# Loading w_down in 7 KB runs, with the gate and up weights read at a column step of 14

## Chip, cores, metric

One core of one Trainium2 chip. The metric is the device time of the whole kernel in microseconds (us), of which every kernel has several runs. Before: 640.87 us median of 4 runs.

## The reference

Two decode layers with shared weights: a GQA attention block over a cache of 8192 positions, and a SwiGLU FFN, run twice. Cut to what matters:

```python
B, D, F = 4, 512, 1792
Hq, Hkv, Sk, Dh = 32, 8, 8192, 128
def _A_ref(x, k_cache, v_cache, wq, wo): ...      # attention; the kernels here read 256 MB, nearly all of it k_cache and v_cache
def _B_ref(x, w_gate, w_up, w_down):
    g = silu(x @ w_gate)                           # w_gate, w_up: [512, 1792]
    u = x @ w_up
    return (g * u) @ w_down                        # w_down: [1792, 512]
x = x + _A_ref(layernorm(x), ...)
x = x + _B_ref(layernorm(x), ...)
x = x + _A_ref(layernorm(x), ...)
x = x + _B_ref(layernorm(x), ...)
```

## The kernel before

The kernel streams both caches once per layer through 11 buffers of 1 MB, except for pieces that it keeps from the first layer for the second, and computes beside the stream. The weights stay in SBUF after one load. Layer 1 is taken batch by batch, so its FFN runs four times inside the stream (each time for all four columns, of which one batch is ready), and once more at the end, for layer 2: five FFNs. A planner in the host code orders the steps of each engine from estimated durations; the order of the loads is a fixed, tuned list.

```python
P, KT, FO = 128, D // 128, F // 128                # 128, 4, 14
def ffn_mm(w_sb, wname, f0, f1, deps, tag):        # gate, and up in two halves
    def fn():
        bk = pbk(tag)
        for fo in range(f0, f1):
            for kt in range(KT):
                op("pe", lambda e: e.matmul(ps[:, bk * BW + (fo - f0) * B:bk * BW + (fo - f0 + 1) * B],
                                            lhsT=w_sb[:, kt, fo * P:(fo + 1) * P],          # stationary: 128 columns
                                            rhs=xnT[:, kt * B:(kt + 1) * B],                # moving: 4 columns
                                            start=(kt == 0), stop=(kt == KT - 1)), ...)
    return PL.add("pe", 0.0295 * KT * (f1 - f0) + 0.05, fn, deps + [...], CHAIN, take=tag, n=2 * KT * (f1 - f0))

def dn(h=h):                                       # down projection, per half
    ...  matmul(..., lhsT=wd_sb[:, fo, nq * P:(nq + 1) * P], rhs=hT[:, fo * B:(fo + 1) * B], ...)

# the loads: what goes where, and the planner's estimate in us
wspec[f"wd{k}"] = (wd_sb[:, fs, :], B_w_down.rearrange("(fo p) n -> p fo n", p=P)[:, fs, :], 2.6)   # k = 0, 1
ORDER = "... a150 wo2 a151 a171 a170 wo3 wu1 wd0 wd1 a160 a161 ..."     # a, b, c: V loads (c: kept for both layers); K: a K load
```

Row f of w_down sits at partition f mod 128, group f // 128, so each partition gets 14 separate rows of 1 KB. hidden(f) must sit at the same place, which is what contiguous blocks of 128 gate and up columns give.

## Time and profile before

| | before |
|---|---|
| time, median of 4 | 640.87 us (639.56 to 641.52) |
| span of the profiled run | 637.9 us |
| bytes read from HBM, rate over the span | 256.1 MB, 402 GB/s |
| TensorE busy, VectorE busy | 63%, 64% |
| DMA packets, of them under 2 KB | 41124, 9816 |

In 36 of the 40 slices of the span the stream moves 400 to 422 GB/s. In few places the rate falls, as in the window 185 to 190 us with its 213 GB/s. The prediction shows the lines. One more is needed that it does not show, the time from issue to landing of all the loads into the stream's buffers (the view of one tile; us, shortest, median, longest):

```profile
DMA to landing us min/median/max: 5.0/10.5/28.1
```

The shortest, 5.0 us, is the first load of the kernel (issued at 0.74 us), which finds nothing ahead of it. So of the median only some 5.5 us is queue, an estimate from these two numbers.

### The profile page before, as it was taken

How to read it: one execution, taken by the hardware profiler on the slowest of the kernel's cores; microseconds unless marked ns; L12 is line 12 of the kernel's file. 1: busy time of each engine (PE TensorE's matmuls, PEld its weight loads, DVE VectorE, ACT ScalarE, POOL GpSimd, SP SyncE). 2: the span in 40 equal slices, each digit the busy share in tenths (PEclk: the TensorE clock that was granted, in tenths of full speed). 3: DMA queues.
4: the chain of work that ended last, by engine and by line, in shares of the span. 5: the costliest groups of instructions: out<-in, count | busy, mean ns of one | idle time of the engine just before them, and what ended most of it. 6: DMA issues, size and time to landing. Idle time of an engine off the chain costs nothing.

```text
span 637.9 us, 18599 instructions
## 1 busy us (share of the span) xinstructions
PE 401.5 (63%) x8657; PEld 202.0 (32%) x8657; DVE 405.2 (64%) x612; ACT 40.2 (6%) x106; POOL 1.8 (0%) x8
## 2 busy tenths in 40 slices
PE   0376454375686655678565575677656776866676
PEld 0231221123542131145331241343421244721355
DVE  6386853464236958776579765466667864499732
ACT  1000200002000020000100100000100020000200
POOL 1000000000000000000000000000000000000000
PEclk9985585565556686665677677567585578577685
DMA  8999999999989999999999999999999999999991
GB/s 362 420 418 407 407 418 420 418 421 400 388 354 422 420 418 420 421 418 404 417 414 418 420 419 421 419 409 411 417 420 420 403 420 420 420 416 420 421 415 42
DMA packets 41124, 257.31 MB, mean 403 GB/s; under 512 B 3924, under 2 KB 9816, under 8 KB 11096
## 3 DMA queue, kind: packets, MB, share of 16 engines
q1 hardware_dynamic: 41048, 256.14, 97.8%
q8 instruction: 67, 1.10, 0.7%
q14 instruction: 9, 0.07, 0.0%
HBM read 256.12 MB, written 0.00 MB: 402 GB/s over the span
## 4 chain that ended last, share of the span: by engine, by line
DMA 64%; PE 16%; DVE 13%; SPq 3%; issue 2%; ACT 0%
DMA pool<-in_A_k_cache_dram 45%; DMA pool<-in_A_v_cache_dram 12%; DVE pool L589 9%; PE ps L605 8%; DMA wq_sb<-in_A_k_cache_dram 5%; PE ps L746 4%; SPq L92 3%; DMA wq_sb<-in_A_v_cache_dram 3%; PE ps L467 1%; DVE negm L624 1%; DVE wq_sb L589 1%; PE ps L792 1%; PE ps L664 1%; PE ps L845 1%; DVE ps L773 1%
## 5 line engine op out<-in xcount | busy, mean ns | idle before, releaser
L589 DVE STREAM_TRANSPOSE pool<-pool 128x2048 uint32<-128x2048 uint32 x116 | 267.1, 2308 | 88.4 <-DMA pool<-in_A_k_cache_dram 87.9
L605 PE MATMUL ps<-pool,qpad 32*32 32x512 bf16 x3840 | 197.4, 548 | 130.8 <-DVE pool L589 125.6
L605 PEld LDWEIGHTS ps<-pool,qpad 32*32 32x32 bf16 x3840 | 55.5, 110 | 248.4 <-DVE pool L589 185.8
L746 PE MATMUL ps<-pool,pp 128*32 128x256 bf16 x1952 | 100.5, 362 | 37.6 <-DMA pool<-in_A_v_cache_dram 28.9
L746 PEld LDWEIGHTS ps<-pool,pp 128*32 128x32 bf16 x1952 | 56.2, 120 | 76.3 <-DMA pool<-in_A_v_cache_dram 34.9
L773 DVE STREAM_TRANSPOSE ps<-ps 128x256 f32<-128x256 f32 x63 | 28.8, 457 | 67.4 <-PE ps L746 67.1
L628 ACT ACTIVATE pp<-ps,negm 128x512 bf16<-128x512 f32 x32 | 21.6, 686 | 322.8 <-DVE negm L624 300.5
L709 PE MATMUL ps<-oT,wo_sb 128*128 128x4 bf16 x640 | 22.4, 166 | 11.3 <-DVE oT L777 8.4
L709 PEld LDWEIGHTS ps<-oT,wo_sb 128*128 128x128 bf16 x640 | 20.0, 102 | 24.8 <-DVE oT L777 15.8
L624 DVE TENSOR_REDUCE negm<-ps 128x1 f32<-128x512 f32 x32 | 19.9, 683 | 12.4 <-PE ps L605 12.4
L467 PE MATMUL ps<-xnT,wq_sb 128*128 128x4 bf16 x640 | 18.3, 166 | 12.8 <-DMA wq_sb<-in_A_wq_dram 11.5
L467 PEld LDWEIGHTS ps<-xnT,wq_sb 128*128 128x128 bf16 x640 | 17.7, 104 | 15.3 <-DMA wq_sb<-in_A_wq_dram 11.6
L589 DVE STREAM_TRANSPOSE wq_sb<-wq_sb 128x2048 uint32<-128x2048 uint32 x8 | 18.5, 2312 | 1.8 <-DMA wq_sb<-in_A_k_cache_dram 1.8
L605 PE MATMUL ps<-wq_sb,qpad 32*32 32x512 bf16 x256 | 11.8, 492 | 9.1 <-DVE wq_sb L589 9.1
L664 PE MATMUL ps<-ident,pp 128*128 128x128 bf16 x128 | 15.4, 300 | 2.5 <-DVE oT L777 1.1
L453 ACT ACTIVATE lnv<-var,eps_sb 128x4 f32<-128x4 f32 x10 | 3.0, 297 | 221.5 <-DVE var L448 221.5
L664 PEld LDWEIGHTS ps<-ident,pp 128*128 128x128 bf16 x128 | 11.9, 137 | 9.6 <-DVE selw L684 2.9
L775 DVE TENSOR_REDUCE osum<-ps 128x4 f32<-128x32 f32 x63 | 12.1, 192 | 2.2
L777 DVE TENSOR_TENSOR oT<-osum,invL 128x4 bf16<-128x4 f32 x63 | 10.6, 169 | 2.1
L673 ACT ACTIVATE pp<-ps 128x1024 bf16<-128x1024 bf16 x8 | 8.2, 1024 | 30.1 <-PE ps L664 30.1
L845 PE MATMUL ps<-hT,wd_sb 128*128 128x4 bf16 x280 | 8.6, 166 | 1.8 <-issue 1.1
L653 DVE TENSOR_SCALAR pp<-pp,alpha 128x512 bf16<-128x512 bf16 x32 | 9.0, 344 | 1.1 <-ACT alpha L646 1.1
(68 smaller groups left out, 143.4 us busy)
## 6 DMA issues: line engine op xcount, KB each, us to landing
pool<-in_A_k_cache_dram SPq DMA_DIRECT2D x116, 1024.0 KB, 10.2
pool<-in_A_v_cache_dram SPq DMA_DIRECT2D x101, 1024.0 KB, 10.8
wq_sb<-in_A_k_cache_dram SPq DMA_DIRECT2D x8, 1024.0 KB, 14.8
wq_sb<-in_A_v_cache_dram SPq DMA_DIRECT2D x5, 1024.0 KB, 16.2
wq_sb<-in_A_wq_dram SPq DMA_DIRECT2D x1, 4096.0 KB, 20.0
wo_sb<-in_A_wo_dram SPq DMA_DIRECT2D x4, 1024.0 KB, 15.5
wg_sb<-in_B_w_gate_dram SPq DMA_DIRECT2D x2, 896.0 KB, 19.2
wu_sb<-in_B_w_up_dram SPq DMA_DIRECT2D x2, 896.0 KB, 16.9
```

The source lines that it names most:

```text
L92: ins = self.eng[engname].dma_start(out_ap, in_ap)
L467: op("pe", lambda e: e.matmul(ps[:, bk * BW + h * B:bk * BW + (h + 1) * B], lhsT=wq_sb[:, kt, h * Dh:(h + 1) * Dh], rhs=xnT[:, kt * B:(kt ...
L589: op("dve", lambda e: e.transpose(v, v), reads=keys, writes=keys)
L605: op("pe", lambda e: e.matmul(ps[32 * c:32 * (c + 1), a * BW:(a + 1) * BW], lhsT=qpad[rows, qbuf, es_, g, :], rhs=ap[h][rows, :, es_ // 2, ...
L624: op("dve", lambda e: e.tensor_reduce(negm[:, q, a:a + 1], bank(a), AX.X, ALU.max, negate=True), reads=[f"pb{a}"], writes=[f"negm{q}_{a}"])
L628: op("act", lambda e: e.activation(pblk(q)[:, :, a, :], bank(a).rearrange("p (t j) -> p t j", j=32), ACTF.Exp, bias=negm[:, q, a:a + 1], s ...
L664: op("pe", lambda e: e.matmul(stg[:, t * P:(t + 1) * P], lhsT=pp[:, q, blk * P:(blk + 1) * P], rhs=ident[:], is_transpose=True, start=True ...
L709: op("pe", lambda e: e.matmul(ps[:, OPJ * BW + nq * B:OPJ * BW + (nq + 1) * B], lhsT=wo_sb[:, h, nq * P:(nq + 1) * P], rhs=oT[:, l, h, :], ...
L746: op("pe", lambda e: e.matmul(ps[32 * n:32 * (n + 1), bk * BW:bk * BW + 256], lhsT=pp[:, q, col:col + 32], rhs=v[:, 8 * f:8 * (f + 1), 32 ...
L773: op("dve", lambda e: e.transpose(blk, blk), reads=[f"pb{bk}"], writes=[f"pb{bk}"])
L775: op("dve", lambda e: e.tensor_reduce(osum[:], diag, AX.X, ALU.add), reads=[f"pb{bk}"], writes=["osum"])
L845: op("pe", lambda e: e.matmul(ps[:, bk * BW + nq * B:bk * BW + (nq + 1) * B], lhsT=wd_sb[:, fo, nq * P:(nq + 1) * P], rhs=hT[:, fo * B:(fo ...
```

## The change

The intent is fewer, longer DMA runs. If row f of w_down goes to partition f // 14, group f mod 14, each partition's share is one piece of 14 KB, loaded in two runs of 7 KB. The hidden activations must then be numbered the same way, so output partition p of group fo needs column p*14 + fo of the gate and up weights: the stationary operand is read with a step of 14 columns, 28 bytes.

```diff
-                                                    lhsT=w_sb[:, kt, fo * P:(fo + 1) * P],
+                                                    lhsT=w_sb[:, kt, bass.ds(fo, P, step=FO)],
...
-            wspec[f"wd{k}"] = (wd_sb[:, fs, :], B_w_down.rearrange("(fo p) n -> p fo n", p=P)[:, fs, :], 2.6)
+            wspec[f"wd{k}"] = (wd_sb[:, fs, :], B_w_down.rearrange("(p fo) n -> p fo n", p=P)[:, fs, :], 2.2)
```

## The prediction

> **What bounds the kernel now.** I read four views in this order: the page's slices and its chain that ended last, the windows by stage, the timeline of the engines around the first and the last FFN, and the queue's issues.
>
> The page first: the DMA digits are 9 in nearly every slice, and the chain is mostly DMA.
>
> ```profile
> DMA  8999999999989999999999999999999999999991
> ...
> HBM read 256.12 MB, written 0.00 MB: 402 GB/s over the span
> ...
> DMA 64%; PE 16%; DVE 13%; SPq 3%; issue 2%; ACT 0%
> ```
>
> So the kernel streams 256 MB and is bound by that stream. The digit line has two breaks: an 8 in slice 11 (175 to 191 us), and the last slice. Elsewhere, compute can be late by several microseconds without moving the end: the K loads take 10.2 us from issue to landing (page, part 6), about four loads of 2.5 us in flight. The windows show the stream's rate in an ordinary stretch, in the stretch with the 1 KB runs of w_down and of the last part of wo, and in the break (columns: window, length, busy us and count of PE, PEld, DVE, ACT, POOL, then granted clock, DMA share, GB/s):
>
> ```profile
> 158.00:169.00 11.00, 7.71 (x186) 6.00 (x174) 2.83 (x14) 0.52 (x3) 0.00 (x0) 0.50 1.07 369
> 200.00:211.00 11.00, 7.16 (x151) 2.37 (x152) 10.66 (x8) 0.00 (x0) 0.00 (x0) 0.64 1.01 422
> 185.00:190.00 5.00, 4.61 (x83) 1.77 (x90) 3.19 (x4) 0.00 (x0) 0.00 (x0) 0.50 0.61 213
> ```
>
> Two places matter for this change. One is the loads of w_down, issued at 156.9 and 158.3 us, when the stream runs at 369 instead of 422 GB/s. The other is every place where an FFN lies on the path. There are five FFNs (four batches of layer 1, one at the end); the last is after the last load and wholly on the path. Its lines in the timeline (start, duration, both us):
>
> ```profile
> 630.26 1.65 PE L792 MATMUL ps<-xnT,wg_sb 128*128 128x4 bf16 x56 [0.49 <-DVE xnT L442]
> 631.78 1.63 PE L792 MATMUL ps<-xnT,wu_sb 128*128 128x4 bf16 x56
> 631.95 0.22 DVE L812 TENSOR_TENSOR gs<-ps,rstd 128x56 f32<-128x56 f32 x1 [1.48 <-PE ps L792]
> 633.25 0.22 DVE L829 TENSOR_TENSOR us<-us,eneg 128x56 f32<-128x56 f32 x1
> 633.50 0.28 DVE L837 TENSOR_TENSOR hT<-us,ps 128x28 bf16<-128x28 f32 x2
> ```
>
> The reader sees a gate of 56 matmuls in 1.65 us, 29.5 ns each, then the up projection beside the vector chain of the SiLU. Up ends at 633.41, the vector chain at 633.47: they finish together, so whatever lengthens up by more than 0.1 us lengthens the end.
>
> The first FFN (batch 0) lies just before the break. There the query of layer 1, batch 0 is made; all buffers hold keys that wait for it, so the loads run dry:
>
> ```profile
> 166.88 1.81 PE L792 MATMUL ps<-xnT,wg_sb 128*128 128x4 bf16 x56 [0.18 <-DVE m L447]
> 169.10 0.89 PE L792 MATMUL ps<-xnT,wu_sb 128*128 128x4 bf16 x28 [0.40 <-DVE gs L812]
> 170.52 0.91 PE L792 MATMUL ps<-xnT,wu_sb 128*128 128x4 bf16 x28 [0.54 <-DVE hT L837]
> 171.70 0.88 PE L845 MATMUL ps<-hT,wd_sb 128*128 128x4 bf16 x27 [0.28 <-DVE hT L837]
> 173.71 0.93 PE L845 MATMUL ps<-hT,wd_sb 128*128 128x4 bf16 x29 [1.12 <-issue]
> 174.90 1.04 PE L746 MATMUL ps<-pool,pp 128*32 128x256 bf16 x16 [0.26 <-DVE xx L861]
> 176.48 1.04 PE L746 MATMUL ps<-pool,pp 128*32 128x256 bf16 x16 [0.54 <-DMA pool<-in_A_v_cache_dram]
> ```
>
> Its slack: 1.12 us of waiting for nothing shown in the down projection, and 0.54 us for a load of V.
>
> [...] A step of 14 bf16 is 28 bytes[...]. No stationary operand of this trace steps that far (the widest is the identity of L480, step 2), so the trace doesn't show the penalty. [...]
>
> **The change, part by part.**
>
> *w_down's loads.* It removes 1792 runs of 1 KB (14 per partition) and adds 256 of 7 KB; the bytes stay 1.835 MB. At 369 GB/s they take 4.97 us, at 422 they take 4.35 us: 0.6 us less. They are in a full stream, so what follows comes 0.6 us sooner. The author's own plan expects 2 x 0.4 us; I keep 0.6.
>
> *Strided weights.* No instruction is added; 5 x 112 = 560 loads of gate and up weights read 28 bytes apart. The down projection, with its rows renumbered the same way, still reads contiguous columns. [...]
> - Last FFN: [...] less the slack of 0.07: **+2.9 us**, all on the path.
> - First FFN: [...] the first half of up runs beside the vector chain, free; the second half starts after hT[...]. The 1.12 us in the down projection and the 0.54 us for V take perhaps 1.0 of it: **+1.2 us** into the break.
> - The other three: [...] against some 10 us of loads in flight: 0. The fourth lets the wq buffer take loads (issue at 557.98), but the stream stays full there.
>
> *The plan.* The order of instructions is computed from estimated times, and the load time entered for w_down falls from 2.6 to 2.2. Everything behind it in the plan may be ordered a little differently. I can't say the sign: +-1 us, mean 0; the order of loads is fixed.
>
> Sum: 640.5 - 0.6 + 2.9 + 1.2 = 644.0 us.
>
> **The rivals.**
>
> 1. *Stride is free.* Weight loads keep 29.5 ns[...]. [...] Then only the DMA gain is left: 640.5 - 0.6 = 639.9 us.
>
> 2. *Doubling, as above*: 644.0 us.
>
> [...]
>
> 4. *The DMA gain is lost in the break.* If batch 0's query comes no sooner, loads that land 0.6 us earlier only run dry 0.6 us earlier: gain 0. For it: the 2 us of missing transfer there (5 us at 213 of 422 GB/s, so 2.5 us). Against it: the wait for V at 176.48 is a wait for that stream. It moves each of the above up by at most 0.6.
>
> **Range and chances.** I give 0.33 to the free stride, 0.55 to doubling, 0.12 to worse. The middle of these, with the DMA gain partly lost, is 643.5 us. The range from 639.2 (free stride, kind plan) to 648.5 (doubling with 2 us more in the break and an unkind plan) should hold 8 times in 10. Faster by 2% would need 627.7 us; the DMA part can't give 13 us, so 0.01. Slower by 2% is above 653.3 us: 0.07. Within 2%: 0.92.
>
> **What would show each step right or wrong.** DMA packets fall from 41124 by 1536 to about 39588, and the window around 158 to 169 us rises from 369 towards 390 GB/s (w_down is some half of it, wo stays at 1 KB). The gate of the last FFN, 56 matmuls, takes 1.65 us if the stride is free[...]; down must keep 1.65. Time from the gate's start to hT in the last FFN, now 3.24 us, grows by 2.9. The break after 185 us gets deeper by about 1 us. The prediction fails if the weight load's cost is not near a factor of two[...], or if the replanned order moves the stream by more than 1 us elsewhere.

The marked cuts took out what no trace shows: a paragraph on how weight loads work, the working of the terms for the strided loads that rested on it, with the added time of the three FFNs in between, what was said for and against the first rival, the third rival (the stride costs about four times), and the test figures that came from these. The sum came to 640.5 - 0.6 + 2.9 + 1.2 = 644.0 us. Of it, +2.9 for the last FFN and +1.2 for the first (where gate and the second half of up were to become longer, and the waits to take 1.0 of that) come from an assumption, that the strided load takes about twice as long; no trace of the kernel before shows it. Without these two terms the sum is 639.9 us.

## The result

650.55 us (648.78 to 652.42, 4 runs) against 640.87: slower by 1.54%, with an interval of 1.19 to 1.89%. A ratio here is the mean time of one kernel's fast runs over that of the other's fast runs of the same rounds, so it isn't quite the ratio of the medians quoted. The time lies 2 us above the predicted range.

Instruction for instruction the two kernels are the same on TensorE, VectorE, ScalarE and GpSimd; only the two loads differ in shape. The smaller number given to the planner moved nothing.

The page of the changed kernel (the DMA digits are tenths of busy time in 40 slices of 16 us, GB/s is the stream's rate in the same slices):

```profile
DMA  8999999999979999999999999999999999999990
GB/s 360 420 417 408 406 418 420 418 420 394 418 298 422 421 420 418 421 399 392 408 412 417 421 419 420 419 400 358 422 405 419 420 421 419 364 413 421 420 407 12
DMA packets 39589, 257.33 MB, mean 398 GB/s; under 512 B 3924, under 2 KB 8024, under 8 KB 9560
...
DMA 60%; PE 25%; DVE 12%; issue 2%; SPq 1%; ACT 0%; DVEq 0%
```

The packets fell as predicted. The chain of work that ended last now has 25% TensorE in place of 16%. The digit of slice 11 is 7 in place of 8; the other holes don't reach the digits, but the row of GB/s has them: counted from 0, slices 17, 18, 27 and 34 (the FFNs of batches 1, 1, 2 and 3) moved 399, 392, 358 and 364, where the page before has 418, 404, 411 and 420. The windows of the same stretches (columns as in the prediction; the last is GB/s):

```profile
158.00:169.00 11.00, 8.04 (x165) 6.49 (x158) 2.60 (x12) 0.50 (x2) 0.00 (x0) 0.50 1.04 397
...
185.00:190.00 5.00, 4.23 (x100) 1.91 (x97) 2.90 (x4) 0.00 (x0) 0.00 (x0) 0.51 0.39 118
```

w_down's stretch rose from 369 to 397 GB/s, and the break fell from 213 to 118. The last FFN in the timeline (start, duration in us):

```profile
635.67 3.52 PE L792 MATMUL ps<-xnT,wg_sb 128*128 128x4 bf16 x56 [0.49 <-DVE xnT L442]
639.05 3.50 PE L792 MATMUL ps<-xnT,wu_sb 128*128 128x4 bf16 x56
...
640.52 0.22 DVE L829 TENSOR_TENSOR us<-us,eneg 128x56 f32<-128x56 f32 x1
...
642.59 0.18 DVE L837 TENSOR_TENSOR hT<-us,ps 128x28 bf16<-128x28 f32 x1 [1.43 <-PE ps L792]
```

Gate and up take twice as long. Up now ends 1.8 us after the vector chain, which waits for it. From the gate's start to the end of the second hT it is 7.10 us in place of 3.52: 3.6 us more. The first FFN:

```profile
166.91 3.49 PE L792 MATMUL ps<-xnT,wg_sb 128*128 128x4 bf16 x56 [0.18 <-DVE m L447]
170.81 1.81 PE L792 MATMUL ps<-xnT,wu_sb 128*128 128x4 bf16 x28 [0.40 <-DVE gs L812]
172.97 1.84 PE L792 MATMUL ps<-xnT,wu_sb 128*128 128x4 bf16 x28 [0.35 <-DVE hT L837]
175.09 1.65 PE L845 MATMUL ps<-hT,wd_sb 128*128 128x4 bf16 x56 [0.28 <-DVE hT L837]
```

The down projection keeps its 1.65 us (0.88 and 0.93 before, around a wait), and the wait of 1.12 us inside it is gone; e2 and e6, with the same stride there, don't have it either. The first half of up was not free: from the gate's end to the start of the second half it is 2.57 us in place of 1.83.

**Where the 9 us went.** From the DMA records of each trace one can read when the n-th megabyte had landed. The table gives how much later than in the kernel before that was, counted from 40 MB on, at five marks: between w_down and the break of batch 0 (74 MB), past that break (100), and past the stretches of the FFNs of batches 1, 2 and 3 (150, 222, 254). One profile per kernel. The first and fifth experiments have the same instructions up to the end of the stream and differ by about 1 us, so a difference of 1 us says nothing; the spans of the kernel before in other runs differ by up to 2.5 us (637.3 to 639.8).

| kernel | before the break | batch 0 | batch 1 | batch 2 | batch 3 |
|---|---|---|---|---|---|
| changed | -0.6 | +1.3 | +3.0 | +5.2 | +7.4 |
| e1, DMA half only | -0.8 | +0.5 | +1.3 | +1.1 | +1.3 |
| e2, stride half only | +0.1 | +2.2 | +4.0 | +4.8 | +8.2 |
| e5, stride in the last FFN only | -0.8 | -0.6 | +0.4 | -0.1 | +0.4 |
| e6, stride in the other four only | -0.6 | +2.4 | +4.5 | +6.1 | +8.6 |
| e7, doubled contiguous | +1.5 | +4.7 | +7.1 | +9.5 | +13.5 |

For the changed kernel: -0.6 from w_down, then +1.9, +1.7, +2.2, +2.2 at the four FFNs in the stream, together +7.4. The last gate starts only 5.4 us later (630.26 to 635.67): some 2 us come back as the stream runs out, where the kernel before has a slow tail (windows of 1 us from 621: 360, 217, 201, 172 GB/s) and the changed one a shorter one (from 629: 373, 287, 115). Why that tail is shorter was not tested. With the last FFN's 3.6 us this makes 9.0 of the 9.1 us between the two spans.

So the FFNs of batches 1 to 3, for which the prediction had put down nothing, took some 6 us. The split among the three is within the scatter, but the sum is not: it is 6.1, 6.0 and 6.2 us in the three kernels with step 14 there (changed, e2, e6), and 0.8, 0.0, 1.0 and 2.3 in e1, e4, e5 and e12 (e4 and e12 read from their traces in the same way), whose weight loads are fast there. Batch 2 shows how. TensorE before and after:

```profile
427.28 1.65 PE L792 MATMUL ps<-xnT,wg_sb 128*128 128x4 bf16 x56
428.80 0.89 PE L792 MATMUL ps<-xnT,wu_sb 128*128 128x4 bf16 x28
429.61 1.04 PE L746 MATMUL ps<-pool,pp 128*32 128x256 bf16 x16
```

```profile
430.06 3.53 PE L792 MATMUL ps<-xnT,wg_sb 128*128 128x4 bf16 x56
433.45 1.82 PE L792 MATMUL ps<-xnT,wu_sb 128*128 128x4 bf16 x28
435.20 1.05 PE L746 MATMUL ps<-pool,pp 128*32 128x256 bf16 x16
```

L746 is a V step; when it ends (436.25 us in the changed kernel), a buffer is free and the next load is issued. The queue that issues, before and after:

```profile
427.44 0.33 SPq L92 DMA_DIRECT2D pool<-in_A_k_cache_dram  x1
430.75 0.33 SPq L92 DMA_DIRECT2D pool<-in_A_v_cache_dram  x1
433.13 0.33 SPq L92 DMA_DIRECT2D pool<-in_A_k_cache_dram  x1
```

```profile
430.22 0.33 SPq L92 DMA_DIRECT2D pool<-in_A_k_cache_dram  x1
436.34 0.33 SPq L92 DMA_DIRECT2D pool<-in_A_v_cache_dram  x1
438.20 0.33 SPq L92 DMA_DIRECT2D pool<-in_A_k_cache_dram  x1
```

In both kernels' order the V step stands behind the gate and the first half of up. The gap between two loads grew from 3.3 to 6.1 us, while a load is moved in 2.5 (1 MB at the 422 GB/s of the ordinary stretch, an estimate). The loads issued between 424 and 437 us took 8.6 us to land in the kernel before, of which 5.0 is what a load takes with nothing ahead of it: some 3.6 us of queue, an estimate from these two. Against it stand 2.8 us more of TensorE before this V step (5.14 us from the gate's start to it, in place of 2.33), and 0.9 more with the second half of up. The stream was already short there (336 GB/s in the window 433 to 434); in the changed kernel it falls to 270 and 213 GB/s at 436 to 438. Batches 1 and 3 have the same pattern: the gap between two loads grows from 3.4 to 5.1 us (issue at 287.08 us in the changed kernel) and from 2.6 to 4.4 us (issue at 553.93 us). There the loads of the kernel before took 8.2 us (V, batch 1) and 9.7 us (K, batch 3) to land, so at batch 3 the same estimate gives 4.7 us of queue; that 2.2 us were lost there all the same is not worked out here.

### The profile page after: what moved, and what is told of

Same layout as the page of the kernel before. It is cut to its first block, busy times and chain, and to the rows that moved or that the text cites. A ratio compares the mean times of both kernels' runs of the same rounds, so it can differ in the third digit from the quotient of the medians.

```text
span 647.0 us, 18599 instructions
## 1 busy us (share of the span) xinstructions
PE 418.7 (65%) x8657; PEld 223.8 (35%) x8657; DVE 405.4 (63%) x612; ACT 40.2 (6%) x106; POOL 1.8 (0%) x8
## 4 chain that ended last, share of the span: by engine, by line
DMA 60%; PE 25%; DVE 12%; issue 2%; SPq 1%; ACT 0%; DVEq 0%
DMA pool<-in_A_k_cache_dram 37%; DMA pool<-in_A_v_cache_dram 14%; PE ps L605 10%; DVE pool L589 8%; PE ps L746 6%; PE ps L792 5%; DMA wq_sb<-in_A_k_cache_dram 4%; DMA wq_sb<-in_A_v_cache_dram 2%; DMA wo_sb<-in_A_wo_dram 2%; PE ps L467 1%; PE ps L845 1%; DVE negm L624 1%; SPq L92 1%; PE ps L709 1%; DVE wq_sb L589 1%
## 5 line engine op out<-in xcount | busy, mean ns | idle before, releaser
L605 PE MATMUL ps<-pool,qpad 32*32 32x512 bf16 x3840 | 193.4, 541 | 125.2 <-DVE pool L589 122.4
L605 PEld LDWEIGHTS ps<-pool,qpad 32*32 32x32 bf16 x3840 | 56.8, 109 | 237.9 <-DVE pool L589 178.8
L746 PE MATMUL ps<-pool,pp 128*32 128x256 bf16 x1952 | 103.0, 370 | 41.4 <-DMA pool<-in_A_v_cache_dram 31.9
L746 PEld LDWEIGHTS ps<-pool,pp 128*32 128x32 bf16 x1952 | 57.5, 122 | 79.9 <-DMA pool<-in_A_v_cache_dram 37.5
L792 PEld LDWEIGHTS ps<-xnT,wu_sb 128*128 128x128 bf16 x280 | 17.6, 160 | 3.8 <-issue 1.3
L792 PE MATMUL ps<-xnT,wu_sb 128*128 128x4 bf16 x280 | 18.2, 199 | 0.8 <-DVE gs L812 0.4
L792 PEld LDWEIGHTS ps<-xnT,wg_sb 128*128 128x128 bf16 x280 | 17.2, 160 | 2.5 <-issue 1.5
L792 PE MATMUL ps<-xnT,wg_sb 128*128 128x4 bf16 x280 | 17.6, 199 | 0.7 <-DVE xnT L442 0.5
L605 PE MATMUL ps<-wq_sb,qpad 32*32 32x512 bf16 x256 | 11.7, 488 | 8.8 <-DVE wq_sb L589 8.8
```

The lines of the kernel that those rows point to most:

```text
L605: op("pe", lambda e: e.matmul(ps[32 * c:32 * (c + 1), a * BW:(a + 1) * BW], lhsT=qpad[rows, qbuf, es_, g, :], rhs=ap[h][rows, :, es_ // 2, ...
L746: op("pe", lambda e: e.matmul(ps[32 * n:32 * (n + 1), bk * BW:bk * BW + 256], lhsT=pp[:, q, col:col + 32], rhs=v[:, 8 * f:8 * (f + 1), 32 ...
```

## The experiments

The theory: the whole loss is the weight load, 27 to 60 ns per product, and it costs the end at all five FFNs. The rivals: the new loads disturb the stream; strided reads of SBUF slow the landing DMA; the order made for other durations is to blame.

### e1 and e2: each half alone

Each is wrong in its results, as the rows no longer match; the instructions are valid.

```diff
# e1: the changed kernel with
+  lhsT=w_sb[:, kt, fo * P:(fo + 1) * P],
# e2: the kernel before with
+  lhsT=w_sb[:, kt, bass.ds(fo, P, step=FO)],
```

> The DMA half alone: w_down in 7 KB runs, gate and up read contiguously (the rows no longer match, so the result is wrong on purpose; the times are valid). Theory (all of the loss is the strided weight load, the DMA half gains 0.6 to 0.7 us): 0.999 of before, 640.2 us; gate of the last FFN 1.65 us, packets 39589. Rival (the new load itself disturbs the stream or the order of the loads that follow): 1.005 or more, 644 us and up.

> The stride half alone: gate and up read with a column step of 14, w_down loaded as before in 1 KB runs (wrong result on purpose). Theory: the whole loss plus the lost gain, 650.6 + 0.7 = 651.3 us, 1.016 of before; gate of the last FFN 3.4 us. Rival (the two halves act together): within 0.4% of before.

e1: 640.60 us, 1.0001 of before (0.9984 to 1.0018). e2: 651.22 us, 1.0169 (1.0150 to 1.0187). The stride half is all of the loss. The DMA half does no harm, and its expected 0.6 us can't be seen in the time. In e1's trace the stream is 0.8 us ahead before the break and 0.5 us behind after the break. The break ends when batch 0's query is there (in the kernel before the load queue waits there for 9.5 us, until a score step of L605 with that query has freed a buffer); loads that land sooner then only run dry sooner, as I read it. In e5, e8 and e12, which have the same or equally fast instructions there, the lead survived (-0.6 to -0.7 us), in e4 it was lost as in e1 (+0.8): TensorE waited for nothing shown for 0.5, 0.6 and 0.8 us inside batch 0's down projection in the first three, and for 1.0 us in e4 and e1. One profile of each is too few to say more than that half a microsecond is lost or kept there by chance.

### e3 and e4: other steps with the same product

```diff
# e3: rows h*896 + p*7 + j, still 7 KB runs
+  lhsT=w_sb[:, kt, bass.ds((fo // 7) * 7 * P + fo % 7, P, step=7)],
+  B_w_down.rearrange("(h p j) n -> h p j n", p=P, h=2)[k]
# e4: rows q*256 + p*2 + r, 2 KB runs
+  lhsT=w_sb[:, kt, bass.ds((fo // 2) * 2 * P + fo % 2, P, step=2)],
+  wd_sb[:, fs, :].rearrange("p (q r) n -> p q (r n)", r=2), B_w_down.rearrange("(q p r) n -> p q (r n)", p=P, r=2)[:, qs, :]
```

What the two theories and the rival below gave as their reason is cut, as no run shows it. The line theory says that a step of 7 costs almost as much as 14, and a step of 2 nothing; the packing theory, that any step costs what 14 costs; the rival, that a step of 7 is free.

> Rows numbered h*896 + p*7 + j: w_down still comes in 7 KB runs, but the gate and up weights are read with a column step of 7 (14 bytes). Result right. Line theory [...] almost as slow as step 14, pitch 56 to 61 ns, 649 to 650.5 us. Packing theory [...]: the same pitch, 61 ns. Rival [...]: pitch 29.5 ns, 640.2 us, equal to or a little faster than before.

> Rows numbered q*256 + p*2 + r: w_down in 2 KB runs (896 packets in place of 1792), gate and up read with a column step of 2 (4 bytes). Result right. Line theory: [...] pitch stays 29.5 ns, time 0.3 to 0.6 us below before, 640.3 us. Packing theory: pitch about 61 ns as at step 14, 650 us.

e3: 646.80 us, 1.0099 (1.0084 to 1.0114), correct; faster than both of its theories said and slower than its rival. e4: 640.13 us, 0.9990 (0.9972 to 1.0008), correct. The last gate in e3, then in e4:

```profile
634.69 3.15 PE L792 MATMUL ps<-xnT,wg_sb 128*128 128x4 bf16 x56 [0.49 <-DVE xnT L442]
```

```profile
630.86 1.65 PE L792 MATMUL ps<-xnT,wg_sb 128*128 128x4 bf16 x56 [0.49 <-DVE xnT L442]
```

A step of 2 is free here (27 ns from start to start, as in the kernel before), so it isn't the mere presence of a step that costs. Step 7 reads 53 ns from start to start, step 14 reads 60. (Here and below a pitch is the median from start to start in the trace. Dividing 1.65 us by 56, as the prediction did, gives 29.5 ns because it contains the 166 ns of the last matmul; the pitch before is 27.0 ns.) In the stream e3 fell back 0.2 us at batch 1, 1.0 at batch 2 and 2.1 at batch 3, where step 14 lost 1.7, 2.2 and 2.2. A fifth less of added hold (26 ns in place of 33) took more than half of the loss at two of the three, which would fit a queue that is just about used up; with 1 us of scatter it is a hint.

### e5 and e6: which FFNs

```diff
# e5, in the changed kernel; e6 has != in place of ==
+  lhsT=w_sb[:, kt, bass.ds(fo, P, step=FO) if tag[0] == "z" else slice(fo * P, (fo + 1) * P)],   # "z": the last FFN
```

Their outputs are wrong, which doesn't matter for the times.

> The changed kernel with the column step of 14 kept in the last FFN only; the four FFNs inside the stream read contiguously (wrong result on purpose). Theory (each FFN costs where it stands): only the tail's 112 x 32 ns = 3.6 us stay, 640.7 + 3.6 = 644.3 us, 1.0055 of before; the stream follows that of the DMA half alone. Prediction's view that the tail and the first FFN carry all: 646 us or more, since the 5.5 us left over have no other home.

> The reverse: step 14 in the four FFNs inside the stream, contiguous in the last (wrong result on purpose). Theory: 650.6 - 3.6 = 647.0 us, 1.010 of before; the stream is held up about 2 us at each of batches 0, 2 and 3 and a little over 1 us at batch 1. The prediction's own step (the three later FFNs cost nothing, the first 1.2 us): 641.5 to 642 us.

e5: 643.66 us, 1.0050 (1.0028 to 1.0073). e6: 647.90 us, 1.0111 (1.0094 to 1.0128). The two losses, 3.2 and 7.1 us of 640.6, add up to 10.3, against 10.8 for the stride alone (e2). This settles the division: a third in the tail, two thirds in the stream. The prediction's step for the three FFNs in the stream is refuted by e6 (7.1 us, where it gave 641.5 to 642 us, some 1 us) together with its row of the table, by which 6.2 us of the delay fall after batch 0.

### e7: the same hold of TensorE without a stride

```diff
# in the kernel before: each accumulation twice, the second overwrites the first
-                    for kt in range(KT):
+                    for kt in [k for _ in range(2) for k in range(KT)]:
```

> The kernel before, contiguous weights and 1 KB runs, but each accumulation of gate and up is done twice, the second writing over the first (right result): 2 x 29.5 = 59 ns of TensorE per product in place of 62. Theory (only the time that TensorE is held counts): 649 to 651 us, as with the stride. Rival (strided reads of SBUF themselves slow the landing DMA): the tail's 3.5 us and little in the stream, 644 to 645 us.

654.37 us, 1.0209 (1.0193 to 1.0224), correct. More than either theory said. The timeline of batch 0 shows a part of why:

```profile
173.50 0.91 PE L792 MATMUL ps<-xnT,wu_sb 128*128 128x4 bf16 x29 [2.08 <-issue]
...
179.69 0.51 PE L845 MATMUL ps<-hT,wd_sb 128*128 128x4 bf16 x13 [1.69 <-issue]
```

With twice the instructions TensorE twice waits for nothing that the profile shows, 3.8 us together, which the strided version with half the instructions doesn't. A third such wait, of 1.49 us, lies in batch 1's up. So e7 is not a clean copy of the hold, and its loss can't be compared with the stride's to the microsecond. What it still says: contiguous weights that hold TensorE as long lose no less in the stream. That strided reads slow the landing DMA can be looked at more directly: while the changed kernel's strided gates of batches 0, 1, 2 and 3 ran, the stream moved 424, 424, 388 and 424 GB/s (the windows 166.9 to 170.4, 281.9 to 285.3, 430.1 to 433.5 and 549.4 to 552.8), where the kernel before has 422 in the ordinary stretch and 379 beside batch 2's gate. So no such slowing is seen.

### e8: a ladder of steps

```diff
+STEPS = {'f0g': 1, 'f0u': 3, 'f1g': 2, 'f1u': 4, 'f2g': 5, 'f2u': 6, 'f3g': 8, 'f3u': 10, 'zg': 12, 'zu': 14}
+  lhsT=w_sb[:, kt, bass.ds(fo, P, step=STEPS[...])],     # one step per gate and per up; wrong on purpose
```

> One look: a different column step for gate and up of each of the five FFNs: 1 and 3, 2 and 4, 5 and 6, 8 and 10, 12 and 14 (wrong result on purpose, no timing meant; only the pitch of the matmuls is read). Line theory, as drawn from steps 2, 7 and 14 (29.5, 55.5, 62 ns): steps 1 to 4 stay at 29.5 ns [...], 5 to 7 lie between [...], 8 and above all cost 62 ns. Smooth theory (cost grows with the step): 3 and 4 already slower, 8 less than 10 less than 12 less than 14.

No timing. Timeline lines of batch 0's gate (step 1), one half of batch 1's up (4), batch 2's gate (5) and batch 3's gate (8):

```profile
166.96 1.63 PE L793 MATMUL ps<-xnT,wg_sb 128*128 128x4 bf16 x56 [0.18 <-DVE m L448]
...
288.52 1.08 PE L793 MATMUL ps<-xnT,wu_sb 128*128 128x4 bf16 x28
...
426.84 2.40 PE L793 MATMUL ps<-xnT,wg_sb 128*128 128x4 bf16 x56
...
542.93 3.53 PE L793 MATMUL ps<-xnT,wg_sb 128*128 128x4 bf16 x56
```

| step (columns of 2 bytes) | 1 | 2 | 3 | 4 | 5 | 6 | 7 (e3) | 8 | 10 | 12 | 14 |
|---|---|---|---|---|---|---|---|---|---|---|---|
| pitch, ns | 27 | 27 | 27 | 33 | 40 | 47 | 53 | 60 | 58 | 59 | 60 |

From 3 to 8 each step adds 6 or 7 ns; below 3 and above 8 the pitch is flat within 2 ns. The rise ends where neighbouring columns lie 16 bytes apart (step 8); what in the hardware makes this shape is not shown. Nor is what sets the flat 27 ns at small steps: without a step it is 25 ns in the half of up at 432.95 us of the kernel before, where the granted clock averaged 0.87 (window 432.95 to 433.8), and 27 where it was 0.50 (gate at 280.35), while step 14 takes 60 ns at 0.96 (gate at 281.8 us of the changed kernel) as at 0.50 (gate at 635.7). The line theory's shape is right, but the point from which it rises was not: I had expected steps up to 4 to be free, and 4 already costs 6 ns. (In e8 each step but 1 stands in one FFN only.) The smooth theory (8, 10, 12 and 14 ever slower) is out.

### e9, e10 and e11: can a better order win it back?

```diff
# e9: the changed kernel, the planner told the true pitch
-            return PL.add("pe", 0.0295 * KT * (f1 - f0) + 0.05, fn, ...
+            return PL.add("pe", 0.060 * KT * (f1 - f0) + 0.14, fn, ...
# e10: that, and for batches 1 to 3 pieces of two groups with the lowest priority; e11: the same pieces in the kernel before, with its 0.0295
+            yields = tag[:2] in ("f1", "f2", "f3")
+            prio, st = ([1e6] if yields else CHAIN), None
+            for a in range(f0, f1, 2 if yields else f1 - f0):
+                z = min(f1, a + 2) if yields else f1
+                st = PL.add("pe", 0.060 * KT * (z - a) + ..., lambda a=a, z=z: fn(a, z), deps + [st, ...], prio, ...)
```

> The changed kernel, with the planner told what the strided gate and up cost on the chip (60 ns per product in place of 29.5); it then orders TensorE anew from batch 1 on (result right). Theory (TensorE held for 3.4 us longer per FFN is what costs, whatever the order): within 2 us of the changed kernel, 648.5 to 652.5 us. Rival (the loss in the stream is only an order made for wrong durations): the in-stream 7 us mostly return, 644 to 645 us.

> The changed kernel, told the true pitch, and gate and up of the FFNs of batches 1 to 3 cut into pieces of two column groups that give way to any score or V step that is ready (result right). Theory (between batches 1 and 3 the loss comes from steps that free buffers standing behind a long FFN [...]): their 5 to 6 us shrink to 2 or less, 645 to 647 us; the break of batch 0 and the tail stay. Rival (the loss comes from the FFN's own chain, that is from the query being late): no better than the changed kernel, 650 us or more.

> The control: the kernel before with the same pieces that give way, contiguous weights, the plan's old durations (result right). Theory: FFNs of 1.65 us hold up little, so within 1.5 us of before, 639.5 to 642 us. If it gains 3 us or more, giving way is worth something by itself and the gain of the yielding changed kernel says little about the stride.

e9: 661.27 us, 1.0327 (1.0312 to 1.0343). e10: 662.04 us, 1.0334 (1.0312 to 1.0356). e11: 645.31 us, 1.0083 (1.0065 to 1.0101). All correct, all worse than the kernels they came from, and none as expected: e9 and e10 missed on both theories, and e11 lost 5 us where I had expected none.

e9 was meant to show that the order doesn't matter. It matters a great deal. Its VectorE at the break of batch 0:

```profile
182.93 0.23 DVE L530 TENSOR_SCALAR qT<-ps,qscale 128x16 bf16<-128x16 f32 x1 [0.92 <-PE ps L467]
185.45 2.31 DVE L589 STREAM_TRANSPOSE pool<-pool 128x2048 uint32<-128x2048 uint32 x1 [2.28 <-DMA pool<-in_A_k_cache_dram]
187.69 0.19 DVE L530 TENSOR_SCALAR qT<-ps,qscale 128x16 bf16<-128x16 f32 x1
```

The new plan puts the transpose of a K load between the two halves of the query, and on the chip that transpose waits for its load. The second half of the query comes at 187.69 us; in the changed kernel, with both halves ahead of the transpose, at 185.14. The stream is 3.3 us behind after this break, not 1.3 (3.4 in e10, which has the same exchange), and up to there this exchange on VectorE is the only change of order. It is 2 us of the 12 by which e9 is further behind at 254 MB than the changed kernel (19.6 and 7.4); where the other 10 went was not traced.

e10 shows the other side of the same FFNs. Letting V and score steps pass does close the first hole: at 126 MB, landed at 312 us with the FFN just done, it is 3.2 us behind, as after the break (3.4). But the FFN ends later, and with it comes the query of batch 1:

```profile
315.77 0.46 PE L480 MATMUL ps<-qT,ident 128*32 128x16 bf16 x16
```

In the changed kernel the same step starts at 306.67. After it the stream falls to 98 GB/s at 334 to 336 us, which I read as buffers full of keys that waited for this query. e11, with cheap weights, does the same: its query comes at 312.13 in place of 304.01, and it loses 5.9 us between 126 and 140 MB, which is all of its loss in the stream. This fits an FFN in the stream that is held from two sides: if it goes first, the steps that free buffers wait for it; if it gives way, the query is late. The theory I had for e10 (only the first side counts) falls, and so does its rival (only the second). Since e9 and e10 change the whole order, they don't prove that no order could hide the added 3.7 us (112 times 33 ns); a search of the list of loads for the new durations was not tried.

### e12: the widest free step

```diff
# rows in blocks: 12 groups in runs of 3 KB, 2 groups in runs of 2 KB; w_down in three loads
+  lhsT=w_sb[:, kt, bass.ds(3 * P * (fo // 3) + fo % 3, P, step=3) if fo < 12 else bass.ds(12 * P + fo - 12, P, step=2)],
```

> The widest free step: rows numbered in blocks so that w_down comes in runs of 3 KB (12 of the 14 column groups) and 2 KB (the last 2), gate and up read with steps of 3 and 2 (result right). Line theory: pitch 27 ns in all gate and up groups; packets fall by 1152; the stream gains about 0.5 us at w_down, of which the break after batch 0 keeps all or nothing, so 0.9985 to 1.001 of before, 639.7 to 641.2 us. If it is below 0.998 the DMA half is worth taking in this form.

640.62 us, 1.0001 (0.9987 to 1.0014) over five rounds, correct. The weight loads stay at 27 ns (a load's own record takes 105 to 106 ns, median, against 104 before and 160 at step 14) and the loads of w_down land in 11.7 us (median; they are three smaller ones) in place of 12.6, and the time is that of before. The stream is 0.7 us ahead past the break and 1.5 us behind past batch 1; why was not traced. With e1 and e4 this is the third form of the DMA half that gains nothing measurable, so no version here beats the kernel before.

## Why the prediction was wrong

Point by point, predicted and measured:

- **The DMA half, -0.6 us.** Right in the stream (-0.6 before the break, 369 to 397 GB/s), worth nothing in the time: e1 is at 1.0001. Its fourth rival, a gain of 0, was right in the number. That the break swallows it is seen in e1 and e4 only; in e5 and e12 the lead outlives the break and is gone past batch 1.
- **The weight load about doubles.** Right in kind, but an assumption that no trace had shown. The true pitches are 27 and 60 ns, so 33 ns more.
- **The last FFN, +2.9 us.** The mechanism was right: up passes the vector chain and all of it is on the path. Measured 3.6 us, which is 112 times 33 ns less the slack; e5 alone shows 3.2 us in the time (its interval goes from 1.8 to 4.7).
- **The first FFN, +1.2 us.** The stream fell back 1.9 us there. The wait in the down projection went, as said, but the first half of up, put down as free, cost 0.7 us.
- **The other three: "against some 10 us of loads in flight: 0".** This is the step that failed. They cost 1.7, 2.2 and 2.2 us. The 10 us was a median over the whole kernel from issue to landing, and I took it as reserve. Half of it is what a load takes with nothing ahead of it (5.0 us), and near these FFNs the loads took 8.2 to 9.7 us to land. At batch 2, with 8.6 us, that left some 3.6 us against an FFN 3.7 us longer, in a place where the stream already ran short by itself; that the other two went the same way is argued from the same pattern of issues, and batch 3's estimate doesn't come out. The digit 9 of a slice hid this: it means 90% or more of 16 us, so a hole of 1.5 us doesn't show; the row of GB/s under it does dip at such a hole.
- **The plan.** It didn't move at all. e9 shows that when it does move it can cost more than the change itself.

The sum had 2.9 + 1.2 - 0.6 = +3.5 us; the spans show 3.6 + 1.9 + 6.1 - 0.6 - 2.0 = +9.0, the last term being what the end of the stream gave back.

## What to carry to other kernels

A layout that makes a load's runs longer can move its cost into every later read: the two loads of w_down, 1.8 MB together, got half a microsecond cheaper, and 560 weight loads dearer by 33 ns each. Before trusting that a full stream hides a delay, look at the queue in that very place, subtract what a load takes alone from its time to landing, and compare windows of 1 us, or at least the rate in each slice, not the digits. And a step of up to 3 bf16 columns in a stationary operand cost no measurable time here (27 ns per product at steps 1, 2 and 3; e4 and e12 took 0.9990 and 1.0001 of before), so it is worth looking for a layout in such a form.
